# Seven block products in place of eight for the product with w_out, and two PSUM banks for the transform

## The chip, the cores and the metric

The kernel runs on one core of one Trainium2 chip. The metric is the device time of one execution in microseconds (us). The engines are named as the profile names them: PE (TensorE, matmuls; PEld its weight loads), DVE (VectorE), ACT (ScalarE), POOL (GpSimd, idle here) and SP (SyncE, which issues the transfers).

## The reference

`x` is 8 batches of 3008 tokens of 256 values, `w_in` is 256 x 2048, `w_out` is 2048 x 256.

```python
X = np.fft.rfft(x, axis=1)
Yr = Xr @ w_r - Xi @ w_i + b_r
Yi = Xr @ w_i + Xi @ w_r + b_i
Yr = sign(Yr) * max(abs(Yr) - 0.01, 0)          # Yi likewise
y = np.fft.irfft(Yr + 1j * Yi, n=3008, axis=1)
h = max(y.reshape(24064, 256) @ w_in, 0)
out = h * h @ w_out
```

## The kernel before

3008 = 47 x 64, so the transform of a batch is made of products with small tables. Stage A (`fft_a`) does the 47 points in 13 groups: `f` is folded on DVE, split into `fh` and `fl`, multiplied into `psa`, copied by ACT to `eva` and sent to a scratch in DRAM. Stage B (`fft_b`) reads it back in 12 pairs of residues per batch: `psb` is the 64-point product, `x` its copy with a sum, split into `xh` (ACT) and `xl` (DVE); the mix with w_r and w_i fills `psm1` and `psm2`; DVE makes `e` out of them in two steps, then `t` and `z` (the threshold, four pieces), and ACT and DVE the parts `zh` and `zl`; `psc` is the 64-point product back, which ACT copies to `evc` for a second scratch. The inverse 47 points (`inverse`) take two groups per chunk of tokens: `psd`, then `dv` (ACT), two pieces of `dx` (DVE) and the parts `xt`.

A float32 operand that goes through PE is split exactly into two float32r parts, `hi` on ACT and `lo` on DVE (`split`), and a product is three matmuls (`mm3`, lines L179 to L181): hi hi, lo hi and hi lo. The first batch, which has PE to itself, uses plain float32 instead.

The tokens come in 52 chunks, 48 with 470 columns and 4 with 376. For each chunk there are 16 hidden blocks `f` of 128. `moe_mm1` multiplies with w_in into the PSUM tile `ph` (6 matmuls); ACT applies relu (L484), DVE squares (L485), and `split` gives `gh` (L173) and `gl` (L174). `moe_mm2` adds the block's product with w_out to `po`, two tiles of 128 outputs (6 matmuls); it stands two blocks behind `moe_mm1` (`LAG`). After the last block `moe_out` copies `po` out, one half on ACT and one on DVE.

Each engine works through its own queue in the order of the program. That order is made by the loop over `f`: the products of the block, then pieces of the next batch's transform in the measure of the matmul time that is due (`active`, `spans`), then the product of the block two before. PSUM has eight banks: four for the transform (`ps_f`), two for `ph` (`ps_h`, one bank each, so two blocks in flight) and two for `po` (`ps_o`).

Of the kernel before, what the change touches and what calls it, by code (L numbers as in the profile page):

```python
# [30 lines left out]
P = 128  # L31
# [9 lines left out]
W = 5  # L41
# [7 lines left out]
# Upper words of 2^-127 and of float32's largest value as float64, read as float32.  # L49
# [4 lines left out]
def groups_of(b):  # L54
    """The small group comes last in an even batch and first in an odd one, so that two meet."""
    return GROUPS if b % 2 == 0 else GROUPS[-1:] + GROUPS[:-1]


def token_order(b):
    """Position in the sequence of each column: by group of n2, n1 = 0..23, then n1 = 46..24."""  # L60
    n1 = np.r_[np.arange(NR), N1 - np.arange(1, NR)]
    return np.concatenate([((64 * n1[:, None] + 47 * (g + np.arange(w))) % S).reshape(-1) for g, w in groups_of(b)])


def folded_rows():
    """Positions in the sequence that are added and subtracted, by group: n1 and 47 - n1; -1 for none."""
    n1 = np.arange(NR)[:, None]
    out = []
    for g, w in GROUPS:
        n2 = g + np.arange(w)  # L70
        a = (64 * n1 + 47 * n2) % S
        b = np.where(n1 > 0, (64 * (N1 - n1) + 47 * n2) % S, -1)
        out.append(np.stack([a, b], 2).reshape(NR * w, 2))
    return out


def _cs(num, den):
    """cos and sin of 2 pi num / den, exact at the multiples of a quarter turn."""
# [8 lines left out]
def tables():  # L87
    """Transform matrices; they depend on the shapes alone."""
# [41 lines left out]

@with_exitstack
def fft_mix_moe(ctx: ExitStack, tc: tile.TileContext, xp, w_r, w_i, b_r, b_i,
# [5 lines left out]
    sb = ctx.enter_context(tc.tile_pool(name="sb", bufs=2))  # L138
# [3 lines left out]
    ps_o = ctx.enter_context(tc.tile_pool(name="ps_o", bufs=1, space=bass.MemoryType.PSUM))  # L142

# [32 lines left out]
    def mm3(out, lt, rt, start, stop):  # L176
        """out (+)= (lt0 + lt1)^T (rt0 + rt1) in float32, by parts that one pass carries each."""
        (l0, l1), (r0, r1) = lt, rt
        nc.tensor.matmul(out, l0, r0, start=start, stop=False)  # L179
        nc.tensor.matmul(out, l0, r1, start=False, stop=False)  # L180
        nc.tensor.matmul(out, l1, r0, start=False, stop=stop)  # L181
# [43 lines left out]
    def load_w(src, dst_hi, dst_lo):  # L225
        """Yields once between the load and the work."""
        h = sb.tile([P, 512], F32, tag="zl", name="w32", bufs=2)
# [3 lines left out]
        else:  # L231
            t = sb.tile([P, 512, 2], U32, tag="xl", name="w64", bufs=2)
# [7 lines left out]
        split(h, dst_hi, dst_lo)  # L240

    def load_win():
        for c in range(DFF // 512):
            for k in range(2):
                s = slice(512 * c, 512 * c + 512)
                yield load_w(w_in[k * P:(k + 1) * P, s], wi_[0][:, k, s], wi_[1][:, k, s])

    def load_wout():
        wo_.extend(ctile(f"wo{k}", [P, NF, D], F32R) for k in range(2))
        wv = w_out.rearrange("(f p) e -> p f e", p=P)  # L250
        for f in range(0, NF, 2):
            s = slice(f, f + 2)
            yield load_w(wv[:, s, :], wo_[0][:, s, :].rearrange("p f e -> p (f e)"),
                         wo_[1][:, s, :].rearrange("p f e -> p (f e)"))

    def rolling(pieces, depth):
        """Runs the pieces one per step, their loads `depth` steps ahead."""
        q = []
        for p in pieces:
            next(p)  # L260
            q.append(p)
            if len(q) > depth:
                for _ in q.pop(0):
                    pass
                yield
        while q:
            for _ in q.pop(0):
                pass
            yield

    def ahead(n, load, depth):
        """Loads of units 0..n-1, each emitted `depth` units before its use."""
# [7 lines left out]
    # `whole`: float32 operands as they are, in the four passes of a float32 product; the first  # L280
    # batch has the tensor engine to itself, and the vector engine is spared the splits.
    def fft_a(b, whole):
# [20 lines left out]
        it = ahead(len(GROUPS), load, 6 if whole else 2)  # L303
        first = next(it)
        yield 0
        for i, t in itertools.chain([first], it):
# [3 lines left out]
            f = sb.tile([P, 512], F32, tag="fold", name="f", bufs=2)[:n]  # L310
# [3 lines left out]
            if not whole:  # L314
                fh = sb.tile([P, 512], F32R, tag="sh", name="fh", bufs=2)[:n]
                fl = sb.tile([P, 512], F32R, tag="sl", name="fl", bufs=2)[:n]
# [8 lines left out]
            if b == 0 and i % 2:  # L325
                e = sb.tile([P, 512], F32, tag="gh", name="eva", bufs=3)[:n]
# [6 lines left out]
    def fft_b(b, whole):  # L333
# [9 lines left out]
        xs, zs = {}, {}  # L343

        def stage_b(i, t):
            tv = t.rearrange("p q (k m) -> p q k m", k=2)
            ps = pst("psb").rearrange("p (k s q t) -> p k s q t", k=2, s=2, q=2)
            for k in range(2):
# [4 lines left out]
                yield 4 * 262  # L353
            x = sb.tile([P, 3, 2, P], F32, tag="x", name="x", bufs=2)
            nc.scalar.copy(x[:, 0:2].rearrange("p s k m -> p k s m"),
                           ps.rearrange("p k s q t -> p k s (q t)"))
            nc.vector.tensor_add(x[:, 2], x[:, 0], x[:, 1])
            if whole:
                xs[i] = x
            else:  # L360
                xh = sb.tile([P, 3, 2, P], F32R, tag="xh", name="xh", bufs=2)
                xl = sb.tile([P, 3, 2, P], F32R, tag="xl", name="xl", bufs=2)
# [3 lines left out]
        def stage_mix(i):  # L366
            x = xs.pop(i)
            p1, p2 = pst("psm1"), pst("psm2")
            for comp, mat, o in ((2, 0, p1[:, :D]), (1, 1, p2[:, :D]), (0, 2, p2[:, D:])):
                for k in range(2):  # L370
# [5 lines left out]
                    yield 3 * 262  # L376
# [251 lines left out]
```

## Time and profile before

| | |
|---|---|
| runs | 2694.63 us median of 3 (2693.78 to 2696.19) |
| profiled execution: span | 2694.1 us; the profile gives no other time of it |
| granted PE clock | 0.996 on average |
| first product of the tokens | starts at 123.7 us |
| HBM | 163.44 MB moved, 61 GB/s on average |

A row of a group gives line, engine, operation, out<-in by the program's names, shapes and count, then busy time, mean ns of one, and idle time of the engine before it with what ended it. A row of the timeline gives start in us, duration, engine, line and operation. A row of the chain gives start, duration and what stood there. A row of the waits says who waited for whom: us in total, times, the longest. Matmuls are pipelined: the recorded duration of one is longer than the distance to the next.

### The profile page before, as it was taken

Reading aid. Unit: us, or ns where it says so; the run is one execution under the profiler, and the core shown is the slowest. Engines: PE = TensorE matmul, PEld = TensorE weight load, DVE = VectorE, ACT = ScalarE, POOL = GpSimd, SP = SyncE. Lnnn points to the kernel's source line nnn. Section 1 sums busy time; section 2 is a strip of 40 time slices with the busy share of each in tenths; the row PEclk is TensorE's granted clock in tenths of the full one; section 3 lists DMA queues with packets and bytes.
Section 4 is the critical chain, followed back from the end, with each engine's and each line's share of the span. In section 5 each row is a group of like instructions: output and inputs, shape, how many; then the busy total and the mean of one; then the engine's idle time right before and its main releaser. Section 6 shows DMA issues by size and latency. Waiting matters only on the chain.

```text
span 2694.1 us, 37380 instructions
## 1 busy us (share of the span) xinstructions
PE 2655.6 (99%) x14088; PEld 2387.3 (89%) x14088; DVE 1841.4 (68%) x3375; ACT 1434.1 (53%) x2649; POOL 0.2 (0%) x4
## 2 busy tenths in 40 slices
PE   6899999999999999999999999999999999999999
PEld 5689989989899898998989989899899989899888
DVE  5877766767667777667676776666767677655555
ACT  5755555545555555555555554555555555444444
POOL 0000000000000000000000000000000000000000
PEclk8999999999999999999999999999999999999999
DMA  8621122111221113211032110321103211100000
GB/s 239 203 69 50 45 87 75 45 40 35 79 89 43 45 34 97 75 39 49 27 97 70 46 52 21 107 68 42 49 20 107 70 43 34 47 31 21 8 15 15
DMA packets 113240, 163.44 MB, mean 61 GB/s; under 512 B 9267, under 2 KB 72995, under 8 KB 113059
## 3 DMA queue, kind: packets, MB, share of 16 engines
q1 hardware_dynamic: 113059, 161.05, 19.3%
q8 instruction: 111, 1.82, 0.3%
q14 instruction: 70, 0.57, 0.1%
HBM read 86.04 MB, written 74.97 MB: 60 GB/s over the span
## 4 chain that ended last, share of the span: by engine, by line
PE 95%; DMA 2%; DVE 1%; ACT 1%; issue 0%; SPq 0%; ACTq 0%; DVEq 0%
PE po L179 13%; PE ph L179 13%; PE po L180 13%; PE ph L180 13%; PE po L181 13%; PE ph L181 13%; PE psd L464 3%; PE psb L351 3%; PE psm L181 2%; PE psm L179 2%; PE psm L180 2%; PE psc L180 1%; PE psc L179 1%; PE psa L179 1%; PE psa L180 1%; PE psa L181 1%
## 5 line engine op out<-in xcount | busy, mean ns | idle before, releaser
L484 ACT ACTIVATE g<-ph 128x470 f32<-128x470 f32 (+1 forms) x832 | 463.0, 557 | 636.1 <-PE ph L181 633.1
L485 DVE TENSOR_TENSOR g<-g 128x470 f32<-128x470 f32 (+1 forms) x832 | 532.2, 640 | 355.1 <-ACT g L484 351.8
L174 DVE TENSOR_TENSOR gl<-g,gh 128x470 fp32r<-128x470 f32 (+1 forms) x832 | 532.2, 640 | 310.7 <-ACT gh L173 300.3
L173 ACT CAST gh<-g 128x470 fp32r<-128x470 f32 (+1 forms) x832 | 483.6, 581 | 416.4 <-DVE g L485 411.6
L179 PE MATMUL po<-gh,wo 128*128 128x470 f32 (+1 forms) x1664 | 644.7, 388 | 0.6
L179 PE MATMUL ph<-xt,wi 128*128 128x470 f32 (+1 forms) x1664 | 622.1, 374 | 1.2 <-ACT xt L173 1.2
L180 PE MATMUL po<-gl,wo 128*128 128x470 f32 (+1 forms) x1664 | 621.5, 374 | 0.0
L180 PE MATMUL ph<-xt,wi 128*128 128x470 f32 (+1 forms) x1664 | 620.4, 373 | 0.0
L181 PE MATMUL po<-gh,wo 128*128 128x470 f32 (+1 forms) x1664 | 619.9, 373 | 0.0
L181 PE MATMUL ph<-xt,wi 128*128 128x470 f32 (+1 forms) x1664 | 617.5, 371 | 0.0
L179 PEld LDWEIGHTS ph<-xt,wi 128*128 128x128 f32 x1664 | 314.3, 189 | 39.4 <-ACT xt L173 1.6
L181 PEld LDWEIGHTS po<-gh,wo 128*128 128x128 f32 x1664 | 314.0, 189 | 38.9
L180 PEld LDWEIGHTS ph<-xt,wi 128*128 128x128 f32 x1664 | 315.8, 190 | 36.4
L181 PEld LDWEIGHTS ph<-xt,wi 128*128 128x128 f32 x1664 | 313.1, 188 | 38.4
L179 PEld LDWEIGHTS po<-gh,wo 128*128 128x128 f32 x1664 | 314.7, 189 | 30.0 <-DVE o L499 2.9
L180 PEld LDWEIGHTS po<-gl,wo 128*128 128x128 f32 x1664 | 315.0, 189 | 26.1 <-DVE gl L174 0.6
L398 DVE TENSOR_TENSOR z<-e,t 64x256 f32<-64x256 f32 x336 | 140.9, 419 | 8.1
L179 PE MATMUL psm<-wm,xh 128*128 128x256 f32 x504 | 143.6, 285 | 0.0
L181 PE MATMUL psm<-wm,xl 128*128 128x256 f32 x504 | 142.3, 282 | 0.0
L180 PE MATMUL psm<-wm,xh 128*128 128x256 f32 x504 | 142.1, 282 | 0.0
L464 PE MATMUL psd<-tD,din 120*128 120x120 f32 (+1 forms) x832 | 126.4, 275 | 5.6 <-DMA din<-s 5.6
L351 PEld LDWEIGHTS psb<-tB,bin 128*128 128x128 f32 x768 | 109.4, 194 | 24.0 <-ACT tMs L173 13.6
(75 smaller groups left out, 2317.0 us busy)
## 6 DMA issues: line engine op xcount, KB each, us to landing
bin<-s SPq DMA_DIRECT2D x96, 256.0 KB
s<-evc SPq DMA_DIRECT2D x96, 256.0 KB
s<-eva SPq DMA_DIRECT2D x96, 240.0 KB
din<-s SPq DMA_DIRECT2D x96, 240.0 KB
outT_dram<-o SPq DMA_DIRECT2D x96, 235.0 KB
xin<-in_xp_dram SPq DMA_DIRECT2D x84, 240.0 KB
w<-in_moe_w_in_dram SPq DMA_DIRECT2D x8, 512.0 KB
w<-in_moe_w_out_dram SPq DMA_DIRECT2D x8, 512.0 KB
```

Source lines behind the costliest of these rows:

```text
L173: nc.scalar.copy(hi, src)
L174: nc.vector.tensor_sub(lo, src, hi.bitcast(F32))
L179: nc.tensor.matmul(out, l0, r0, start=start, stop=False)
L180: nc.tensor.matmul(out, l0, r1, start=False, stop=False)
L181: nc.tensor.matmul(out, l1, r0, start=False, stop=stop)
L351: nc.tensor.matmul(ps[:, k, :, q, :], tv[:, q, k], tB[:, 0:r + 2:r + 1], start=True, stop=True)
L398: nc.vector.tensor_sub(z[64 * c:64 * c + 64, q], e[src, c], t[src, c])
L464: nc.tensor.matmul(ps[:, k, part], t[:, s:s + P], tD[:n, tab + part, :n], start=True, stop=True)
L484: nc.scalar.activation(g[:, :n], ph[:, :n], AF.Relu)
L485: nc.vector.tensor_mul(g[:, :n], g[:, :n], g[:, :n])
```

## The change

Two hidden blocks are now one unit `j` (`NU` = 8 per chunk). The unit's product with w_out is a product of two by two blocks: two halves of the tokens (236 and 234 columns, which share two; 188 and 188 in a small chunk) by two blocks of hidden values, and those by two halves of the outputs. It is computed by Winograd's form of Strassen's scheme, with seven block products. Their right operands are made of w_out once (`load_wout`, seven tiles per unit); their left operands `g` are four squared blocks of which three are replaced or joined by sums, with three subtractions on DVE. The seven products add up over the units of a chunk in four PSUM banks, two to a bank (`PLACES`), and are combined in `moe_out` by seven DVE instructions, which now gives four output transfers per chunk instead of two.

`ph` of a unit takes two banks and has one buffer. The transform has two banks (`ps_f`) instead of four; before the tokens' products begin it borrows `po`'s (`pst`). Square is done by ACT. Many SBUF pools are halved or shared (`tmp`, `x`, `zh`, `zl`, `xh`), and in stage B the split of `x` and the threshold are separate steps. `fill` brings in the transform's pieces twice per unit.

```diff
-    ps_f = ctx.enter_context(tc.tile_pool(name="ps_f", bufs=4, space=bass.MemoryType.PSUM))
-    ps_h = ctx.enter_context(tc.tile_pool(name="ps_h", bufs=2, space=bass.MemoryType.PSUM))
+    ps_f = ctx.enter_context(tc.tile_pool(name="ps_f", bufs=2, space=bass.MemoryType.PSUM))
+    ps_h = ctx.enter_context(tc.tile_pool(name="ps_h", bufs=1, space=bass.MemoryType.PSUM))
...
+PLACES = ((0, 0, 0), (2, 0, 1), (6, 1, 0), (5, 1, 1), (4, 2, 0), (3, 2, 1), (1, 3, 0))
+    def opnd(tag, name, dt):
+        return sb.tile([P, NPR, HALF], dt, tag=tag, name=name, bufs=2)
     def ldt(name):
-        return sb.tile([P, 512], F32, tag="ld", name=name, bufs=8)
+        return sb.tile([P, 512], F32, tag="ld", name=name, bufs=4)
     def evt(name):
-        return sb.tile([P, 512], F32, tag="ev", name=name, bufs=4)
+        return sb.tile([P, 512], F32, tag="ev", name=name, bufs=2)
...
+                a = h.rearrange("p (f e m) -> p f e m", f=2, e=2)
+                w7 = sb.tile([P, NPR, P], F32, tag="xh", name="w7")
+                nc.scalar.copy(w7[:, 0:3:2], a[:, :, 0])
+                nc.scalar.copy(w7[:, 1], a[:, 1, 1])
+                nc.vector.tensor_add(w7[:, 4], a[:, 0, 1], a[:, 1, 1])
+                nc.vector.tensor_sub(w7[:, 6], w7[:, 4], a[:, 0, 0])
+                nc.vector.tensor_sub(w7[:, 5], a[:, 0, 0], a[:, 0, 1])
+                nc.vector.tensor_sub(w7[:, 3], a[:, 1, 0], w7[:, 6])
+                split(w7, wo_[0][:, j], wo_[1][:, j])
...
+    def hidden(ph, n):
+        m, t0 = halves(n)
+        g = opnd("g", "g", F32)
+        b4 = g[:, 0:4, :m]
+        for t in range(2):
+            nc.scalar.activation(g[:, t:4:2, :m], ph[:, :, t * t0:t * t0 + m], AF.Relu)
+        nc.scalar.activation(b4, b4, AF.Square)
+        nc.vector.tensor_sub(g[:, 4:6, :m], g[:, 1:4:2, :m], g[:, 0:2, :m])
+        nc.vector.tensor_sub(g[:, 6, :m], g[:, 3, :m], g[:, 4, :m])
+        nc.vector.tensor_sub(g[:, 1, :m], g[:, 6, :m], g[:, 2, :m])
+        return g
+    def parts(g, n):
+        m, _ = halves(n)
+        gh, gl = opnd("gh", "gh", F32R), opnd("gl", "gl", F32R)
+        split(g[:, :, :m], gh[:, :, :m], gl[:, :, :m])
+        return gh, gl
-    def moe_mm2(po, gg, n, f):
-        for k in range(2):
-            es = slice(k * P, k * P + P)
-            mm3(po[k][:, :n], (wo_[0][:, f, es], wo_[1][:, f, es]),
-                (gg[0][:, :n], gg[1][:, :n]), f == 0, f == NF - 1)
+    def moe_mm2(po, gg, n, j):
+        m, _ = halves(n)
+        for s, bank, half in PLACES:
+            mm3(po[bank][:, half * m:half * m + m], (wo_[0][:, j, s], wo_[1][:, j, s]),
+                (gg[0][:, s, :m], gg[1][:, s, :m]), j == 0 and half == 0, j == NU - 1,
+                skip_group_check=True)
...
+        nc.scalar.copy(p1, p[0])
+        add, sub = nc.vector.tensor_add, nc.vector.tensor_sub
+        add(o[0][:, 0], p[2], p1)
+        add(o[0][:, 1], p[6], p1)
+        add(o[1][:, 0], p[5], o[0][:, 1])
+        add(o[0][:, 1], p[4], o[0][:, 1])
+        add(o[1][:, 1], p[4], o[1][:, 0])
+        add(o[0][:, 1], p[3], o[0][:, 1])
+        sub(o[1][:, 0], o[1][:, 0], p[1])
...
+        for j in range(NU):
+            step = c * NF + 2 * j
+            ph = moe_mm1(xts[c], n, j)
+            g = hidden(ph, n)
+            next(wout, None)
+            fill(step)
+            if len(pend) == LAG:
+                do_mm2()
+            pend.append((c, j, parts(g, n)))
+            fill(step + 1)
```

In the rows that follow, a semaphore is named by the engine that is waited for. DVE's queue before, in the middle of a batch, where the mix of a pair of residues is worked off (L381 the second step of e, L394 t, L398 z, L402 zl, L485 a square, L174 a lower part):

```order
L381 TENSOR_TENSOR e<-psm_11061,e 128x512 [waits PE_49]
L174 TENSOR_TENSOR gl<-g,gh 128x470 [waits Activation_49]
L394 TENSOR_SCALAR t<-e 128x512 [waits DVE_49]
L398 TENSOR_TENSOR z<-e,t 64x256 [waits DVE_49]
L398 TENSOR_TENSOR z<-e,t 64x256 x3
L485 TENSOR_TENSOR g<-g 128x470 [waits Activation_49]
L402 SCALAR_TENSOR_TENSOR zl<-z,sg,zh 128x256 [waits Activation_49] x2
L174 TENSOR_TENSOR gl<-g,gh 128x470 [waits PE_49,Activation_49]
```

The same place after (L430 and L431 e, L207 a lower part, L454 t, L458 z, L462 zl, L560 to L562 the three subtractions of a unit):

```order
L430 TENSOR_TENSOR e<-psm_12871,bias_82 128x512 [waits PE_49]
L207 TENSOR_TENSOR gl<-g,gh 128x1652 [waits Activation_49]
L431 TENSOR_TENSOR e<-psm_12872,e 128x512 [waits DVE_49,PE_49]
L207 TENSOR_TENSOR xl<-x,xh 128x768 [waits Activation_49]
L454 TENSOR_SCALAR t<-e 128x512 [waits DVE_49]
L458 TENSOR_TENSOR z<-e,t 64x256 [waits DVE_49]
L458 TENSOR_TENSOR z<-e,t 64x256 x3
L560 TENSOR_TENSOR g<-g 128x472 [waits Activation_49]
L462 SCALAR_TENSOR_TENSOR zl<-z,sg,zh 128x256 [waits Activation_49] x2
L561 TENSOR_TENSOR g<-g 128x236 [waits DVE_49]
L562 TENSOR_TENSOR g<-g 128x236 [waits DVE_49]
L207 TENSOR_TENSOR gl<-g,gh 128x1652 [waits Activation_49]
```

Where the threshold's pieces stood among short operations of one block each, the whole chain from e to zl now stands between one gl and the last subtraction of the next unit.

ACT's queue before, in the middle of a batch (L484 relu, L173 an upper part, L401 zh, L415 the copy evc):

```order
L484 ACTIVATE g<-ph 128x470 [waits PE_49,Activation_49]
L173 CAST gh<-g 128x470 [waits DVE_49]
L484 ACTIVATE g<-ph 128x470 [waits PE_49,Activation_49]
L401 ACTIVATE zh<-z,sg 128x256 [waits DVE_49]
L415 COPY evc<-psc 128x512 [waits DMAHW1_49,PE_49]
L401 ACTIVATE zh<-z,sg 128x256 [waits DVE_49]
L173 CAST gh<-g 128x470 [waits DVE_49]
```

The same queue after, at the unit of the DVE rows above (L558 relu, L559 square, L206 an upper part, L461 zh):

```order
L206 CAST gh<-g 128x1652 [waits DVE_49,PE_49,Activation_49]
L206 CAST xh<-x 128x768 [waits PE_49]
L558 ACTIVATE g<-ph 128x2x236 [waits PE_49]
L558 ACTIVATE g<-ph 128x2x236
L559 ACTIVATE g<-g 128x944 [waits Activation_49]
L461 ACTIVATE zh<-z,sg 128x256 [waits DVE_49] x2
L206 CAST gh<-g 128x1652 [waits DVE_49,PE_49,Activation_49]
L558 ACTIVATE g<-ph 128x2x236 [waits PE_49]
```

One gh now covers all seven operands of a unit and waits for DVE's subtractions and for the product two units before (PE), and the next unit's relu stands behind it.

More of the change, by code (lines that the diff above doesn't have):

```diff
@@ L160, in fft_mix_moe, with tmp @@
     wo_ = []
+    starting = [True]
+    turn = itertools.count()
     def ldt(name):
-        return sb.tile([P, 512], F32, tag="ld", name=name, bufs=8)
+        return sb.tile([P, 512], F32, tag="ld", name=name, bufs=4)
     def evt(name):
-        return sb.tile([P, 512], F32, tag="ev", name=name, bufs=4)
+        return sb.tile([P, 512], F32, tag="ev", name=name, bufs=2)
+    def tmp(name):
+        return sb.tile([P, 512], F32, tag="tmp", name=name, bufs=2)
     def pst(name):
+        k = next(turn) % 6
+        if starting[0] and k > 1:
+            return ps_o.tile([P, 512], F32, tag=f"o{k - 2}", name=name)
         return ps_f.tile([P, 512], F32, tag="f", name=name)
@@ L239, in load_w @@
             narrow(t, h)
-        split(h, dst_hi, dst_lo)
+        use(h)
     def load_win():
@@ L245, in load_win, with use, rolling @@
                 s = slice(512 * c, 512 * c + 512)
-                yield load_w(w_in[k * P:(k + 1) * P, s], wi_[0][:, k, s], wi_[1][:, k, s])
+                def use(h, k=k, s=s):
+                    split(h, wi_[0][:, k, s], wi_[1][:, k, s])
+                yield load_w(w_in[k * P:(k + 1) * P, s], use)
     def load_wout():
-        wo_.extend(ctile(f"wo{k}", [P, NF, D], F32R) for k in range(2))
+        wo_.extend(ctile(f"wo{k}", [P, NU, NPR, P], F32R) for k in range(2))
         wv = w_out.rearrange("(f p) e -> p f e", p=P)
[L251 to L258, printed above, removed]
+        for j in range(NU):
+            def use(h, j=j):
+                a = h.rearrange("p (f e m) -> p f e m", f=2, e=2)
[7 more added lines that the diff above has]
+                split(w7, wo_[0][:, j], wo_[1][:, j])
+            yield load_w(wv[:, 2 * j:2 * j + 2, :], use)
+    def rolling(pieces):
+        last = None
         for p in pieces:
+            if last is not None:
+                for _ in last:
+                    pass
             next(p)
[L261 to L268, printed above, removed]
+            last = p
             yield
+        for _ in last:
+            pass
+        yield
     def ahead(n, load, depth):
@@ L301, in load @@
                 return st[i // 8][:NR * GROUPS[i][1], i % 8, :]
-        it = ahead(len(GROUPS), load, 6 if whole else 2)
+        it = ahead(len(GROUPS), load, 3 if b == 1 else 2)
         first = next(it)
@@ L324, in fft_a @@
                         (fh[:, cs], fl[:, cs]), True, True)
-            if b == 0 and i % 2:
-                e = sb.tile([P, 512], F32, tag="gh", name="eva", bufs=3)[:n]
+            if b == 0 and i % 3:
+                e = sb.tile([P, NPR * HALF], F32, tag="g", name="eva", bufs=2)[:n, :512]
             else:
@@ L423, in fft_b @@
                 _, t = next(it)
-                yield from stage_b(i, t)
-            if 0 <= i - 1 < NPAIR:
-                yield from stage_mix(i - 1)
+                stage_b(i, t)
+                yield 8 * 262
+            if 0 <= i - 2:
+                stage_c(i - 2)
+                yield 3 * 518
+            e = None
+            if 0 <= i - 1 < NPAIR:
+                e = stage_mix(i - 1)
+            if i < NPAIR:
+                split_x(i)
+            if e is not None:
+                threshold(i - 1, e)
+                yield 18 * 262
             if i >= NPAIR:
                 yield 0
-            if 0 <= i - 2:
-                yield from stage_c(i - 2)
     GAP = 8
@@ L489, in moe_mm2, with moe_mm1 @@
[L489 to L493 removed]
+            yield 8 * 262
+    def moe_mm1(xt, n, j):
+        ph = ps_h.tile([P, 2, 512], F32, tag="h", name="ph")
+        for a in range(2):
+            f = 2 * j + a
+            fs = slice(f * P, f * P + P)
+            for k in range(2):
+                mm3(ph[:, a, :n], (wi_[0][:, k, fs], wi_[1][:, k, fs]),
+                    (xt[0][:, k, :n], xt[1][:, k, :n]), k == 0, k == 1)
+        return ph
@@ L495, in moe_out @@
     def moe_out(c, po):
         n = cols[c]
+        m, t0 = halves(n)
+        p = {s: po[bank][:, half * m:half * m + m] for s, bank, half in PLACES}
+        p1 = sb.tile([P, HALF], F32, tag="p1", name="p1")[:, :m]
+        o = [sb.tile([P, 2, HALF], F32, tag=f"o{k}", name="o") for k in range(2)]
+        o = [x[:, :, :m] for x in o]
+        nc.scalar.copy(p1, p[0])
+        add, sub = nc.vector.tensor_add, nc.vector.tensor_sub
+        add(o[0][:, 0], p[2], p1)
+        add(o[0][:, 1], p[6], p1)
@@ L553, in fft_mix_moe, with fill @@
     LAG = 2
-    def do_mm2():
-        c, f, gg = pend.pop(0)
-        if f == 0:
-            pos[c] = [ps_o.tile([P, 512], F32, tag=f"o{k}", name=f"po{k}") for k in range(2)]
-        moe_mm2(pos[c], gg, cols[c], f)
-        if f == NF - 1:
+    def fill(step):
+        for b, (s0, s1) in spans.items():
+            if s0 == step:
+                active.append([full(b), s0, s1, 0, A_COST + 1000 * GAP + B_COST])
+        for a in list(active):
+            gen, s0, s1, done, total = a
+            want = total * (step + 1 - s0) / (s1 - s0)
+            while a[3] < want or step >= s1:
+                try:
+                    a[3] += next(gen)
+                except StopIteration:
+                    active.remove(a)
+                    break
+    def do_mm2():
+        c, j, gg = pend.pop(0)
+        if j == 0:
+            pos[c] = [ps_o.tile([P, 512], F32, tag=f"o{k}", name=f"po{k}") for k in range(4)]
+        moe_mm2(pos[c], gg, cols[c], j)
+        if j == NU - 1:
             moe_out(c, pos.pop(c))
```

124 lines of the change are left out of this document (57 added, 67 removed).

## The prediction

> **What bounds the kernel now.** I read the busy shares first, then the chain that ended last, then the waits, then the timeline.
>
> ```profile
> span 2694.1 us, 37380 instructions
> PE 2655.6 (99%) x14088; PEld 2387.3 (89%) x14088; DVE 1841.4 (68%) x3375; ACT 1434.1 (53%) x2649; POOL 0.2 (0%) x4
> ...
> PE 95%; DMA 2%; DVE 1%; ACT 1%; issue 0%; SPq 0%; ACTq 0%; DVEq 0%
> ...
> L179 PE MATMUL ph<-xt,wi x1664: 329/377/482, 123.7 to 2685.5; 128*128 128x470 f32 x170, 128*128 128x376 f32 x15
> ...
> ACT g L484 <- PE ph L181: 633.1, 722, 2.3
> DVE g L485 <- ACT g L484: 351.8, 494, 2.2
> DVE gl L174 <- ACT gh L173: 300.3, 503, 1.0
> ```
>
> PE makes up 95% of the chain; DVE and ACT wait for it and for each other, and both have room. The token products run from 123.7 us to the end. Matmul durations overlap, so PE's price is the distance between starts, or the chain's share of each:
>
> ```profile
> 1003.05 0.37 PE L181 MATMUL ph<-xt,wi 128*128 128x470 f32 x1
> 1003.26 0.28 PE L179 MATMUL psm<-wm,xh 128*128 128x256 f32 x1
> 1003.38 0.28 PE L180 MATMUL psm<-wm,xh 128*128 128x256 f32 x1
> 1003.50 0.28 PE L181 MATMUL psm<-wm,xl 128*128 128x256 f32 x1
> 1003.62 0.38 PE L179 MATMUL po<-gh,wo 128*128 128x470 f32 x1
> ...
> 1010.07 0.23 PE psc L181
> 1010.30 0.44 PE psd L464 x4
> ...
> 180.85 0.89 PE psb L351 x8
> ```
>
> 470 columns cost 0.2125 us, 256 cost 0.118, so 0.44 ns a column and 5 ns beside. By that, 376 columns cost 0.171 us.
>
> I count in units, a pair of hidden blocks f, of which there are 416: 384 with 470 columns, 32 with 376. A unit before is 24 matmuls: 5.10 us, or 4.10 in a small one; together 2089. The transform adds on PE, per pair of residues (84 behind the start), 0.89 + 18 x 0.118 + 3 x 0.23 = 3.7 us, 312; per group of stage A (78) 6 x 0.118 = 0.71, 55; per chunk (52) 16 psd at 0.11 = 1.76, 92. With 124 of start and 8 of end this is 2680 of the 2694.1 us profiled. That execution lies 0.5 us below the runs' median.
>
> **What the change does to PE.** The product with w_out becomes 21 matmuls of 236 columns in place of 12 of 470. By the line above 236 columns cost 0.109 us, so 2.29 us instead of 2.55; in small units 188 columns cost between 0.088 and 0.109, for the weight load need not shrink. PE alone would come to 384 x 4.84 + 32 x 4.15 + 312 + 55 + 92 + 155 = 2606 us. No float32r matmul narrower than 256 stands in this trace; that it keeps to the line is the choice nearest to the row.
>
> **What it does to ACT and DVE.** The durations come from these rows:
>
> ```profile
> L484 ACT ACTIVATE g<-ph 128x470 f32<-128x470 f32 x768 | 432.0, 563 | 600.2 <-PE ph L181 598.0 <-ACT xt L173 0.2
> L173 ACT CAST gh<-g 128x470 fp32r<-128x470 f32 x768 | 451.1, 587 | 381.3 <-DVE g L485 377.3
> L173 ACT CAST xh<-x 128x768 fp32r<-128x768 f32 x84 | 70.1, 835 | 1.7 <-DVE x L357 0.5
> L174 DVE TENSOR_TENSOR gl<-g,gh 128x470 fp32r<-128x470 f32 x768 | 497.0, 647 | 284.9 <-ACT gh L173 276.7 <-PE po L180 2.0 <-PE ph L181 1.3
> L174 DVE TENSOR_TENSOR xl<-x,xh 128x768 fp32r<-128x768 f32 x84 | 80.4, 957 | 10.1 <-ACT xh L173 7.0
> L471 DVE TENSOR_TENSOR dx<-psd,dv 128x230 f32<-128x230 f32 x96 | 37.3, 388 | 0.0
> ...
> 2640.11 0.56 ACT L484 ACTIVATE g<-ph 128x470 f32<-128x470 f32 x1 [0.69 <-PE ph L181]
> 2640.71 0.65 DVE L485 TENSOR_TENSOR g<-g 128x470 f32<-128x470 f32 x1 [0.60 <-ACT g L484]
> 2641.39 0.59 ACT L173 CAST gh<-g 128x470 fp32r<-128x470 f32 x1 [0.72 <-DVE g L485]
> ```
>
> ACT costs 0.832 ns an element more and DVE 1.04; a hand-over between them costs some 0.035 us. Per unit after: two relus of 472 elements, 1.13; the square of 944 moves from DVE to ACT, 587 + 474 x 0.832 = 0.98; the cast gh of 1652, 1.57. On DVE: the three new subtractions, 0.65 + 0.39 + 0.39; gl of 1652, 1.88. So ACT rises from 2.30 to 3.68 us a unit and DVE from 2.59 to 3.31, while PE falls by 0.26.
>
> What decides is the order. In ACT's queue each unit reads relu, relu, square, gh, and the next unit's relu stands behind gh. gh is one instruction over all seven operands, so it waits for the last subtraction, and that for the square. This is a ring: 1.13 + 0.98 + 1.43 + 1.57 = 5.11, five hand-overs add 0.18, neighbours on ACT that overlap take back 0.13 (row at 1010.64 below): **5.16 us a unit**, 4.37 in a small one (relu 0.484 each, the others by the same slopes). PE cannot run ahead of it by more than a unit: there is one pair of PSUM banks for ph, so the next unit's first product waits for this unit's relus. Before, ph had two buffers, and the order relu, gh of one f at a time left ACT idle for 2.55 - 1.15 us each. Units together: 384 x 5.16 + 32 x 4.37 = 2121, which is 32 above PE's 2089 before. Thus the matmuls saved are gone already without any transform.
>
> **The transform inside the ring.** Its rows:
>
> ```profile
> 1008.89 0.42 DVE L394 TENSOR_SCALAR t<-e 128x512 f32<-128x512 f32 x1
> 1009.35 1.74 DVE L398 TENSOR_TENSOR z<-e,t 64x256 f32<-64x256 f32 x4
> 1011.12 0.65 DVE L485 TENSOR_TENSOR g<-g 128x470 f32<-128x470 f32 x1
> 1011.68 0.48 DVE L402 SCALAR_TENSOR_TENSOR zl<-z,sg,zh 128x256 fp32r<-128x256 f32 x1
> ...
> 1010.23 0.51 ACT L401 ACTIVATE zh<-z,sg 128x256 fp32r<-128x256 f32 x1
> 1010.64 0.57 ACT L415 COPY evc<-psc 128x512 f32<-128x512 f32 x1
> ...
> L381 DVE TENSOR_TENSOR e<-psm,e 128x512 f32<-128x512 f32 x96 | 66.1, 688 | 43.1 <-PE psm L181 41.7 <-PE psm L372 1.3
> L355 ACT COPY x<-psb 128x512 f32<-128x512 f32 x96 | 55.9, 582 | 11.7 <-PE psb L351 11.7
> ```
>
> A DVE instruction that waits for nothing starts 0.09 us before its forerunner's recorded end, one on ACT 0.10. In the unit with the mix, DVE's queue reads gl, e, xl, t, four z, first subtraction, two zl, two subtractions; then comes gh. From one start of gh to the next: 1.60 for gh, 1.79 gl, 0.60 e, 0.87 xl, 0.46 t, 1.77 z, 0.56, 0.78 zl, 0.86 with the last hand-over: 9.29 us, 4.13 over the ring. Only the other e lies under gh, at no cost. The copies x and evc stand on ACT between gh and square: 0.48 each. So a pair of residues costs 5.1 us, 428 in all; on PE it cost 3.7, beside which DVE's part was hidden. If all of it hid under DVE's and ACT's idle time it would cost nothing.
>
> ```profile
> L469 ACT COPY dv<-psd 128x240 f32<-128x240 f32 x96 | 34.3, 357 | 21.0 <-PE psd L464 21.0
> L173 ACT CAST xt<-dx 128x470 fp32r<-128x470 f32 x96 | 56.4, 587 | 24.9 <-DVE dx L471 22.2
> L499 DVE COPY o<-po 128x470 f32<-128x470 f32 x48 | 30.9, 643 | 5.4 <-PE po L181 5.4
> L329 ACT COPY eva<-psa 120x512 f32<-120x512 f32 x96 | 56.1, 587 | 29.5 <-PE psa L181 9.8 <-PE psa L321 9.6 <-DMA s<-eva 6.2
> L173 ACT CAST fh<-f 120x512 fp32r<-120x512 f32 x72 | 44.8, 623 | 2.8 <-DVE f L312 2.8
> ```
>
> Each half of the inverse puts two dx between the subtractions and xt ahead of gh: 1.0 us (0 if all under gh, 2.4 if none). Writing out a chunk was one copy on ACT and one on DVE; now it is a copy and seven sums of 236, at 0.43 in a chain, six of them beside gh's 1.6 us: 1.2. A chunk thus costs 3.2, 166 in all. A group of stage A costs ACT 1.0 for fh and eva; its bounds are 0.7 (PE's own) and 2.4, all of DVE's work too, and I take 1.2, near the rows: 94. w_out's seven combinations go through the ring in eight pieces, about 3 us each: 24.
>
> At the start only four buffers in place of seven take stage A's results; three waits like the longest s<-eva, 7 us, would make 21 (0 to 40): 145. SP issues two more output transfers a chunk, which nothing waits for. The half-size pools for ev and ld cost nothing at one eviction in 5 us; otherwise they add to the second rival. The last unit ends with gl, 21 matmuls, the sums and a transfer: 12.
>
> Sum: 145 + 2121 + 428 + 94 + 166 + 24 + 12 = **2990 us**, 11% slower.
>
> **The rivals.**
> - *The work packs well and PE stays the bound*: 2606 us. For it: DVE's 1841 us grow by some 410, ACT's 1434 by about 560, both below 2606. It decides at 2694, where 296 of the 712 us that I charge to transform, chunks and w_out would have to hide in idle time. Against it: queues keep their order, and in the unit with the mix nothing but one e stands under gh.
> - *Two PSUM banks for the transform*: PE stops at psd or psm until DVE has read e, with the next ph queued behind. 1.5 us for each of 84 pairs and 104 psd would give 3270; half of it 3130. PE's slack in the ring speaks against it: 0.3 us in a bare unit, 2.3 in the one with the mix (9.29 against 4.84 + 2.12).
> - *Narrow float32r falls to float32's passes*: the first batch's float32 psm give its price.
>
> ```profile
> 94.81 1.67 PE L372 MATMUL psm<-wmf,x 128*128 128x256 f32 x7
> ...
> L179 PEld LDWEIGHTS psm<-wm,xh 128*128 128x128 f32 x504 | 94.9, 188 | 8.5
> ```
>
> Six starts in 1.30 us, two a product, make 0.43 us for 256 columns, 0.40 for 236: 8.4 us for the 21 instead of 2.29, some 5100 us. No row below 256 excludes it.
> - *Weight loads set the pace*: at 0.188 us one after the other, 8736 loads in place of matmuls at 0.109 would lift PE from 2606 to 3300. The psm rows 0.118 apart, each with its load, speak against it. The Trainium skill, "Perfetto Trace Analysis", section "Identifying the Most-Contended Engine", calls matmul busy time a bad measure and takes the summed time of LDWEIGHTS slices over the window as the good one; by that rule the 17,832 loads after would not fit into the time before. The trace bears it out only in part: 14,088 loads of this length sum to 98% of the span, yet loads overlap each other where matmuls are short.
>
> **How the numbers follow.** The ring, my forecast, gets 0.75, with its own range 2820 to 3130 from the bounds of the pair, the groups and the start. Good packing 0.12, the PSUM banks 0.08, narrow passes 0.03, weight loads 0.02. A range of 2690 to 3180 leaves out the good packing, the last two and a part of the banks, 2 in 10. About 0.2% is what a measurement of this kernel can tell from no change: faster 0.12, the same 0.02, slower 0.86.
>
> **What would show it.** Right: PE's share of the span falls to about 85%, with idle time ahead of ph released by ACT's relu; in the last chunks relus of successive units stand 5.2 us apart; square about 0.98, gh 1.57, gl 1.88 us; gaps of 1.5 us on ACT ahead of gh, ended by the last subtraction; 9 us between gh's around z. Wrong: po starts more than 0.12 us apart, PE at 97% or more, or PE waiting at psd and psm for DVE's e.

## The result and the profile after

The changed kernel takes 3065.5 us (median of 4 runs, 3063.7 to 3065.6) against 2694.6 us for the kernel before, run beside it: 1.137 times as long, with a 95% interval of 1.135 to 1.139. The forecast was 2990 us, with 2690 to 3180 as its range. The profiled execution has a span of 3063.6 us.

In the new kernel's lines L558 is relu, L559 the square, L560 to L562 the three subtractions, L206 the cast to the high part (gh, xh, fh, xt), L207 the subtraction for the low part (gl, xl), L212 to L214 the three matmuls of a product, L461 zh and L458 z. The page begins its parts with the span, the busy shares and the chain that ended last:

```profile
span 3063.6 us, 45137 instructions
...
PE 2758.2 (90%) x17832; PEld 2523.0 (82%) x17832; DVE 2247.4 (73%) x3719; ACT 1914.9 (63%) x2665; POOL 0.2 (0%) x4
...
DVE 39%; ACT 32%; PE 16%; issue 10%; DMA 3%; ACTq 0%; SPq 0%; DVEq 0%
ACT gh L206 14%; ACT g L559 7%; ACT g L558 6%; DVE g L560 6%; DVE gl L207 6%; DVE z L458 4%; DVE g L561 4%; DVE g L562 4%; PE ph L212 2%; DVE xl L207 2%; PE ph L213 2%; PE ph L214 2%; DVE e L431 2%; PE po L212 2%; PE po L214 2%
```

PE's share of the chain fell from 95 to 16%, though PE is still "busy" for 90% of the span: a matmul is drawn 0.27 or 0.37 us long where the next could start 0.111 or 0.2125 us behind it, so a wait shorter than the difference does not show as idle time. The chain now passes through the relus, the square, the three subtractions and gh, which is the order in which a unit goes through them. The waits (us in all, times, longest) name the same members:

```profile
DVE gl L207 <- ACT gh L206: 530.1, 365, 3.4
ACT gh L206 <- DVE g L562: 525.0, 312, 2.8
ACT zh L461 <- DVE z L458: 186.7, 164, 4.1
...
PE ph L212 <- ACT g L558: 71.2, 53, 4.6
PE psa L212 <- ACT fh L206: 52.2, 27, 4.3
ACT eva L375 <- PE psa L214: 50.5, 33, 2.5
...
PE psd L531 <- DVE e L430: 12.3, 8, 2.0
```

ACT waits for DVE's last subtraction and DVE waits for ACT's cast, 525 and 530 us. Each has more than a quarter of the span idle, and each waits for the other. The timeline of a unit without transform, near the end, shows how:

```profile
3000.76 1.58 ACT L206 CAST gh<-g 128x1652 fp32r<-128x1652 f32 x1 [1.68 <-DVE g L562]
3002.23 1.01 ACT L558 ACTIVATE g<-ph 128x472 f32<-128x472 f32 x2
3002.36 1.88 DVE L207 TENSOR_TENSOR gl<-g,gh 128x1652 fp32r<-128x1652 f32 x1 [1.72 <-ACT gh L206]
3003.28 0.99 ACT L559 ACTIVATE g<-g 128x944 f32<-128x944 f32 x1
3004.30 0.65 DVE L560 TENSOR_TENSOR g<-g 128x472 f32<-128x472 f32 x1
3004.99 0.40 DVE L561 TENSOR_TENSOR g<-g 128x236 f32<-128x236 f32 x1
3005.43 0.41 DVE L562 TENSOR_TENSOR g<-g 128x236 f32<-128x236 f32 x1
3005.94 1.57 ACT L206 CAST gh<-g 128x1652 fp32r<-128x1652 f32 x1 [1.67 <-DVE g L562]
```

From gh to gh it is 5.18 us. Leave gl out, and every row starts within 0.11 us of its forerunner's end; the hand-overs go ACT, DVE, ACT. That is the ring; gl alone lies beside it, as does all of PE's work. In a unit with the threshold the same stretch is 9.40 us, because DVE's queue holds other work ahead of the subtractions for which gh waits:

```profile
1004.62 1.57 ACT L206 CAST gh<-g 128x1652 fp32r<-128x1652 f32 x1 [1.67 <-DVE g L562]
...
1006.23 1.88 DVE L207 TENSOR_TENSOR gl<-g,gh 128x1652 fp32r<-128x1652 f32 x1 [1.11 <-ACT gh L206]
1008.02 0.68 DVE L431 TENSOR_TENSOR e<-psm,e 128x512 f32<-128x512 f32 x1
1008.62 0.95 DVE L207 TENSOR_TENSOR xl<-x,xh 128x768 fp32r<-128x768 f32 x1
1009.49 0.42 DVE L454 TENSOR_SCALAR t<-e 128x512 f32<-128x512 f32 x1
1009.94 1.74 DVE L458 TENSOR_TENSOR z<-e,t 64x256 f32<-64x256 f32 x4
1011.71 0.65 DVE L560 TENSOR_TENSOR g<-g 128x472 f32<-128x472 f32 x1
1012.28 0.88 DVE L462 SCALAR_TENSOR_TENSOR zl<-z,sg,zh 128x256 fp32r<-128x256 f32 x2
...
1014.02 1.57 ACT L206 CAST gh<-g 128x1652 fp32r<-128x1652 f32 x1 [1.79 <-DVE g L562]
```

### The profile page after: what moved, and what is told of

It reads as the page before. It is cut to its first block, busy times and chain, and to the rows that moved or that the text cites. A ratio compares the mean times of both kernels' runs of the same rounds, so it can differ in the third digit from the quotient of the medians.

```text
span 3063.6 us, 45137 instructions
## 1 busy us (share of the span) xinstructions
PE 2758.2 (90%) x17832; PEld 2523.0 (82%) x17832; DVE 2247.4 (73%) x3719; ACT 1914.9 (63%) x2665; POOL 0.2 (0%) x4
## 4 chain that ended last, share of the span: by engine, by line
DVE 39%; ACT 32%; PE 16%; issue 10%; DMA 3%; ACTq 0%; SPq 0%; DVEq 0%
ACT gh L206 14%; ACT g L559 7%; ACT g L558 6%; DVE g L560 6%; DVE gl L207 6%; DVE z L458 4%; DVE g L561 4%; DVE g L562 4%; PE ph L212 2%; DVE xl L207 2%; PE ph L213 2%; PE ph L214 2%; DVE e L431 2%; PE po L212 2%; PE po L214 2%
## 5 line engine op out<-in xcount | busy, mean ns | idle before, releaser
L207 DVE TENSOR_TENSOR gl<-g,gh 128x1652 fp32r<-128x1652 f32 (+1 forms) x416 | 770.3, 1852 | 530.1 <-ACT gh L206 530.1
L206 ACT CAST gh<-g 128x1652 fp32r<-128x1652 f32 (+1 forms) x416 | 644.7, 1550 | 585.6 <-DVE g L562 525.0
L212 PE MATMUL po<-gh,wo 128*128 128x236 f32 (+1 forms) x2912 | 827.1, 284 | 34.6 <-DVE o L588 16.8
L213 PE MATMUL po<-gl,wo 128*128 128x236 f32 (+1 forms) x2912 | 813.9, 280 | 3.3 <-DVE gl L207 3.3
L214 PE MATMUL po<-gh,wo 128*128 128x236 f32 (+1 forms) x2912 | 814.6, 280 | 0.0
L212 PE MATMUL ph<-xt,wi 128*128 128x470 f32 (+1 forms) x1664 | 652.6, 392 | 72.0 <-ACT g L558 71.2
L214 PE MATMUL ph<-xt,wi 128*128 128x470 f32 (+1 forms) x1664 | 630.0, 379 | 0.0
L212 PEld LDWEIGHTS po<-gh,wo 128*128 128x128 f32 x2912 | 569.0, 195 | 64.5 <-DVE o L588 19.0
L213 PEld LDWEIGHTS po<-gl,wo 128*128 128x128 f32 x2912 | 569.3, 195 | 11.2 <-DVE gl L207 4.1
L214 PEld LDWEIGHTS po<-gh,wo 128*128 128x128 f32 x2912 | 571.1, 196 | 0.0
L558 ACT ACTIVATE g<-ph 128x472 f32<-128x472 f32 (+1 forms) x832 | 418.3, 554 | 97.3 <-PE ph L214 96.8
L212 PEld LDWEIGHTS ph<-xt,wi 128*128 128x128 f32 x1664 | 322.8, 194 | 123.4 <-ACT g L558 91.5
L559 ACT ACTIVATE g<-g 128x944 f32<-128x944 f32 (+1 forms) x416 | 410.6, 987 | 8.6
L214 PEld LDWEIGHTS ph<-xt,wi 128*128 128x128 f32 x1664 | 322.9, 194 | 40.4
L560 DVE TENSOR_TENSOR g<-g 128x472 f32<-128x472 f32 (+1 forms) x416 | 266.7, 641 | 103.6 <-ACT g L559 93.2
L461 ACT ACTIVATE zh<-z,sg 128x256 fp32r<-128x256 f32 x168 | 85.6, 510 | 186.7 <-DVE z L458 186.7
L212 PE MATMUL psm<-wm,xh 128*128 128x256 f32 x504 | 147.1, 292 | 40.3 <-DVE dx L537 22.5
L562 DVE TENSOR_TENSOR g<-g 128x236 f32<-128x236 f32 (+1 forms) x416 | 165.7, 398 | 11.4
L561 DVE TENSOR_TENSOR g<-g 128x236 f32<-128x236 f32 (+1 forms) x416 | 165.1, 397 | 8.7
L458 DVE TENSOR_TENSOR z<-e,t 64x256 f32<-64x256 f32 x336 | 141.0, 420 | 7.4
```

The lines of the kernel that those rows point to most:

```text
L206: nc.scalar.copy(hi, src)
L207: nc.vector.tensor_sub(lo, src, hi.bitcast(F32))
L212: nc.tensor.matmul(out, l0, r0, start=start, stop=False, **kw)
L213: nc.tensor.matmul(out, l0, r1, start=False, stop=False, **kw)
L214: nc.tensor.matmul(out, l1, r0, start=False, stop=stop, **kw)
L458: nc.vector.tensor_sub(z[64 * c:64 * c + 64, q], e[src, c], t[src, c])
```

## The experiments

Theory: the ring of relu, square, subtractions and gh over two in-order queues sets the pace, and the transform that stands in those queues is added to it. Rivals: PE's own work; the two PSUM banks; the sum of work on ACT and DVE, in whatever order. Each kernel was timed in three rounds beside the kernel before, which measured 2694.4 to 2696.4 us.

**Less work for PE.** The changed kernel with the third matmul of each w_out product left out, so that w_out's low part does not enter the result: 14 matmuls a unit in place of 21.

```
-            mm3(o, (wo_[0].., wo_[1]..), (gg[0].., gg[1]..), ...)
+            nc.tensor.matmul(o, wo_[0].., gg[0].., ...)
+            nc.tensor.matmul(o, wo_[0].., gg[1].., ...)
```

> The changed kernel with one of the three passes left out in the product with w_out (the pass with the low part of w_out), 14 matmuls of 236 columns a unit in place of 21. The output lacks that pass. The ring on ACT and DVE (theory): PE loses 7 x 0.111 = 0.78 us a unit, 320 us of work, but stands in no ring, so a bare unit stays at 5.19 us and the time falls by 0 to 50 us, to 3015 to 3065. PE or the narrow matmuls as the bound (rival): the time falls by some 320 us, to about 2745. Stops at the two PSUM banks (rival): PE's stops at psd and psm stay, the time falls by 100 to 200 us, since PE has less to do behind each stop.

3063.1 us, 1.137 (1.135 to 1.138): no change. The page's busy shares, and one of the waits:

```profile
PE 2534.2 (83%) x14920; PEld 2264.7 (74%) x14920; DVE 2240.8 (73%) x3719; ACT 1913.5 (63%) x2665; POOL 0.2 (0%) x4
```

```profile
PE ph L212 <- ACT g L558: 232.9, 152, 5.1
```

2912 matmuls at 0.111 us, some 320 us of PE's work, went away, and PE's wait for the relus rose from 71 to 233 us. PE is not the bound. The Trainium skill, "Perfetto Trace Analysis", section "Identifying the Most-Contended Engine", prefers the summed weight loads to the matmuls' busy time for telling how near PE is to its limit. This case does not bear that out: the loads' times sum to 99% of the span in the kernel before, to 114% in the changed kernel and to 98% here, and PE is the bound in the first of the three alone (the shares on the page, 89, 82 and 74%, count loads that overlap once).

**The order of the queues.** Two ways to take gh off the ring. In the first, the split of a unit is issued one unit later, behind the next unit's square, so that gh no longer stands between a unit's subtractions and the next relu; g keeps its two buffers:

```
+            if held:
+                pc, pj, pg = held.pop()
...
+                with tc.issue_after(sq):
+                    gg = parts(pg, cols[pc])
...
+            held.append((c, j, g))
```

> The changed kernel with the split into gh and gl put one unit later, behind the next unit's square on ACT; nothing is left out. gh no longer waits for the subtractions of its own unit. g still has two buffers, so the next relu has to wait until gl has read the older one. The ring (theory): the old ring is gone and a new one stands in its place, relu 1.03, square 0.99, gh 1.57, gl 1.88 and hand-overs, 5.55 us in a bare unit in place of 5.19; the time is between 3000 and 3250. The sum of work on ACT and DVE as the bound (rival): the same work, so 3065 and 5.19. PE as the bound (rival): 3065.

3078.4 us, 1.142 (1.141 to 1.144). The timeline near the end, and its largest wait:

```profile
3022.08 1.02 ACT L558 ACTIVATE g<-ph 128x472 f32<-128x472 f32 x2 [2.00 <-DVE gl L207]
3023.13 0.99 ACT L559 ACTIVATE g<-g 128x944 f32<-128x944 f32 x1
3024.03 1.56 ACT L206 CAST gh<-g 128x1652 fp32r<-128x1652 f32 x1
3027.59 1.02 ACT L558 ACTIVATE g<-ph 128x472 f32<-128x472 f32 x2 [2.00 <-DVE gl L207]
```

```profile
ACT g L558 <- DVE gl L207: 611.0, 324, 4.1
```

The old ring is gone, gh follows the square at once, and another took its place: the relu waits until gl has read g two units back. 5.51 us a unit. The same with a third buffer for g (paid for with one load buffer and with p1 in a shared one):

```
-        return sb.tile([P, NPR, HALF], dt, tag=tag, name=name, bufs=2)
+        return sb.tile([P, NPR, HALF], dt, tag=tag, name=name, bufs=3 if tag == "g" else 2)
```

> The same late split with three buffers of g (room for it is made by three load buffers in place of four, two loads ahead at the start in place of three, and p1 among the temporaries), so that neither gh nor the next relu waits for DVE's last step. The ring (theory): no ring is left that is longer than PE's unit of 2.55 + 21 x 0.111 = 4.88 us, and the transform is once more beside PE where DVE keeps up: 2620 to 2800. Two PSUM banks (rival): the transform's stops stay as they are, above 2950. The sum of work on ACT and DVE (rival): unchanged work, 3065. Narrow matmuls (rival): PE no faster than now, 3065.

2841.3 us, 1.054 (1.053 to 1.056): 224 us less than the changed kernel, though 41 us above what I had expected at most. The second way leaves the order and cuts the one cast in four, so that ACT casts the blocks that are ready while DVE still subtracts:

```
-        split(g[:, :, :m], gh[:, :, :m], gl[:, :, :m])
+        for s in (slice(0, 3, 2), slice(3, 6), slice(6, 7), slice(1, 2)):
+            nc.scalar.copy(gh[:, s, :m], g[:, s, :m])
+        nc.vector.tensor_sub(gl[:, :, :m], g[:, :, :m], gh[:, :, :m].bitcast(F32))
```

> The changed kernel with gh cast in four instructions, blocks 0 and 2 first, then 3 to 5, 6, 1, each waiting only for its own subtraction; ACT has about 0.6 us more work a unit. The ring (theory): the casts run beside the subtractions, relu 1.03, square 0.99 and casts 2.3 make 4.3 us, so that a bare unit comes to PE's 4.88, and the unit with z falls from 9.40 to about 8.2: 2820 to 2940. The sum of work on ACT and DVE as the bound (rival): ACT's extra work makes it slower, 3065 to 3300. PE as the bound (rival): 3065.

2809.7 us, 1.042 (1.041 to 1.044), 10 us below the range that I gave, at 148 us more work on ACT. Busy shares and chain, then two relus of its timeline in the last third:

```profile
PE 2658.2 (95%) x17832; PEld 2469.4 (88%) x17832; DVE 2243.4 (80%) x3719; ACT 2063.1 (74%) x3913; POOL 0.2 (0%) x4
...
PE 73%; DVE 14%; ACT 8%; DMA 3%; issue 3%; SPq 0%; DVEq 0%; ACTq 0%
```

```profile
2500.31 1.02 ACT L558 ACTIVATE g<-ph 128x472 f32<-128x472 f32 x2 [0.63 <-PE ph L214]
...
2505.21 1.02 ACT L558 ACTIVATE g<-ph 128x472 f32<-128x472 f32 x2 [0.65 <-PE ph L214]
```

The relus stand 4.90 us apart and wait for PE: 12 x 0.2125 + 21 x 0.111 is 4.88. Three lines, with the same products, banks and sums, give back 256 of the 371 us. That settles the ring, and with it that the sum of work is not the cause: ACT does more here and the kernel is faster.

**The two PSUM banks alone.** The kernel before, with nothing but

```
-    ps_f = ctx.enter_context(tc.tile_pool(name="ps_f", bufs=4, space=bass.MemoryType.PSUM))
+    ps_f = ctx.enter_context(tc.tile_pool(name="ps_f", bufs=2, space=bass.MemoryType.PSUM))
```

> The kernel before, with one thing of the change alone: the transform gets two PSUM banks instead of four, and nothing uses the other two. Ring theory: the banks are a side matter; the new kernel's waits on PE at psd, psb and psm for a reader of a bank sum to some 30 us. With PE as the bound here they cost about that: 2725 us, between 2695 and 2760. Rival (the banks are the cause): 1.5 us for each of 84 pairs and 104 halves of the inverse, or half of it: 2835 to 2975 us.

2703.8 us against 2694.4: 1.004 (1.002 to 1.005). The banks cost 9 us where PE is the bound and the order is that of the kernel before.

**Stage A.** Its price was the worst term of my sum (below). In the changed kernel its split, its products and its eviction were put into three successive steps of the loop:

```
+                split(f, fh, fl)
+                if late:
+                    evict(*late)
+                yield 3 * 262
...
+                late = (g, w, n, o, i)
+                yield 3 * 262
```

> The changed kernel with one edit: stage A's split, products and eviction of a group stand in three successive steps of the loop, so that the eviction no longer stands in ACT's queue right behind the cast whose products it waits for. If ACT's wait for psa (50 us in all) and PE's for fh (52 us) are why a group costs 1.8 us and not the 1.2 that I had taken: 3015 us, between 3000 and 3035. If a group's price is the work on ACT and DVE that stands in the ring, whatever its order: 3055 to 3070 us.

3036.1 us, 1.127 (1.125 to 1.129): 29 us of the 50 expected, just above the range that I gave. Its waits show which part did not come: ACT's for psa fell from 50.5 to 11.8 us, but PE's for fh only from 52.2 to 36.6, its wait for fl rose from 14.6 to 24.4, and fh itself now waits for the products to release its one buffer:

```profile
PE psa L212 <- ACT fh L206: 36.6, 24, 4.3
...
ACT fh L206 <- PE psa L214: 17.3, 18, 2.3
...
ACT eva L359 <- PE psa L214: 11.8, 12, 2.2
```

**Towards the kernel before.** Four versions build on gh in pieces. First all of the transform in smaller portions: stage A as above, and the mix, the split of x and the halves of the threshold each in a step of its own,

```
-                yield 18 * 262
+                yield 6 * 262      (behind the mix)
+                yield 4 * 262      (behind the split of x, and in each half of the threshold)
```

> The cast of gh in four pieces, and the transform handed out in smaller portions: stage A's split, products and eviction in three successive steps, the mix, the split of x and the two halves of the threshold each in a step of their own, with buffers of their own for e and t. If what is left over the pieces' 2810 us is portions that stand together in one unit, stage A falls from 1.8 to about 1.2 us a group (48 us) and some 20 to 30 us go elsewhere: 2740 us, between 2700 and 2780. If what is left is PE's own work (bare unit 4.90, mix 2.14, both near PE's own price), it stays within 2790 to 2815. Neither theory says that it beats the kernel before: 2695 us lies only 90 above PE's own sum.

2821.2 us, 1.047 (1.046 to 1.049), slower than the pieces alone by 11.5 us and above both forecasts. I reckon PE's gaps behind the start from the trace, as the sum over its matmuls of the distance to the next start beyond that kind's own price (0.2125 us for ph, 0.111 for po, 0.118 for psm and psa, and so on), where that is over 0.05. They are 162 us in the run with pieces, 86 of them at psa; here 175, with 63 at psa. (Counted against each kind's median distance instead, they are some 20 us more in every run, with the same differences.) What stage A gave, other places took: ph behind po went from 10 to 25.

Then stage A alone, in steps and with its share of the schedule tripled, so that its groups stand about one in two units:

```
-    A_COST = len(GROUPS) * 6 * 262
+    A_COST = len(GROUPS) * 18 * 262
```

> The pieces of gh, with stage A's three steps, and stage A's share of the schedule tripled, so that its groups stand about one in two units instead of several in one. In the run with pieces PE's gaps beside psa sum to some 85 us behind the start. If these are the crowding of stage A, most of them go: 2740 us, between 2720 and 2770. If a group's price stays wherever it stands, nothing is won: 2795 to 2815 us.

2773.8 us, 1.029 (1.027 to 1.031), 36 us less and 4 above the range. The gaps at psa fell from 86 to 29 us; those within psm rose from 7 to 19, and psc and psb gained 20 beside it. To this was added, in the first batch, that stage A evicts into its own input:

```
-            if b == 0 and i % 3:
-                e = sb.tile([P, NPR * HALF], F32, tag="g", name="eva", bufs=2)[:n, :512]
+            if b == 0:
+                e = load(i)
```

> The same, and in the first batch stage A writes its result over the group's input instead of into one of four shared buffers. The changed kernel's first token product stands 23 us later than before; if the four buffers make that, most of it goes: 15 to 25 us under the run without this. If it is something else of the start, no change. Together with the thin stage A 2720 us, still above the kernel before.

2763.9 us, 1.025 (1.023 to 1.027), 10 us less where I had expected 15 to 25. The first and last ph of the run without it and of this one:

```profile
L212 PE MATMUL ph<-xt,wi x1664: 328/377/954, 150.0 to 2759.8; 128*128 128x470 f32 x170, 128*128 128x376 f32 x15
```

```profile
L212 PE MATMUL ph<-xt,wi x1664: 328/377/954, 138.6 to 2748.2; 128*128 128x470 f32 x170, 128*128 128x376 f32 x15
```

So the buffers make 11 of the 23 to 26 us by which the start is late; the rest is not explained. Last, the fourth step of the transform was issued behind the threshold, with two buffers for zh and zl:

```
-            if 0 <= i - 2:
+            if whole and 0 <= i - 2:
                 stage_c(i - 2)
...
+            if not whole and 0 <= i - 2:
+                stage_c(i - 2)
+                yield 3 * 518
```

> The last one, with the fourth step of the transform (psc, evc) issued behind the threshold instead of ahead of the mix, and two buffers in place of one for zh and zl (and so for fh and fl). In the run before it PE loses some 125 us in gaps behind the start: about 19 between the mix's products, 29 beside psa, 18 ahead of or within psc, 9 behind psb. If buffers and the order of the two banks make these, half goes: 2700 us, between 2680 and 2740; only at the low end does it reach the kernel before. If the queues of ACT and DVE make them, it stays at 2750 to 2770.

2783.5 us, 1.033 (1.031 to 1.035): 20 us slower. The gaps within psm rose from 19 to 30 us, and 13 behind po ahead of it are 7 more than before; the gaps in all from 126 to 147. That lies outside both forecasts. The edit changes the order and the buffers together, so it shows only that this order with these buffers is worse. The waits point to the two banks: PE's waits for a reader of one of the transform's banks rose from some 28 us (psm for evc 14.6, psc for dx 7.6, and smaller ones) to some 50 (psm for dx 14.8, x 9.3 and evc 8.9, psb for evc 12.7, and smaller ones), about as much as the time. Whether the number of banks makes these waits or the queue in which the reader stands, no run separates.

No version beats the kernel before. The best, at 2762.9 us of span, nearly adds up: PE's own 2606, which already holds a later start (the prediction's 155 us for start and end, here 153); 16 because a product of 236 columns takes 0.111 and not 0.109 us; 8 because one of 188 columns in a small chunk takes 0.11 too; and 126 of gaps. That makes 2756, 7 short, as the same sum was 14 short for the kernel before (2680 of 2694). At the measured spacings the units alone fall from 2089 to 2014 us of PE's time, so the seven products save 75 us. The gaps and a start that is 15 us later take 141, which is 66 more; the span is 69 longer. What the seven products take away in slack costs more than they save in every order tried.

## Why the prediction was right, by its steps

- **PE bounds before, the ring after**: right. The run with less work on PE and the one with gh in pieces show it from two sides.
- **The ring's length**: 5.16 us forecast; 5.18 from gh to gh above. The new instructions' sizes came out of the slopes of the old rows (0.98, 1.57 and 1.88 forecast), as the groups by form show:

```profile
L207 DVE TENSOR_TENSOR gl<-g,gh 128x1652 fp32r<-128x1652 f32 x384 | 721.4, 1879 | 499.1 <-ACT gh L206 499.1
L206 ACT CAST gh<-g 128x1652 fp32r<-128x1652 f32 x384 | 603.3, 1571 | 546.5 <-DVE g L562 490.4 <-PE po L214 19.8 <-PE ph L214 12.1
...
L559 ACT ACTIVATE g<-g 128x944 f32<-128x944 f32 x384 | 383.9, 1000 | 7.7
```

- **The unit with the mix**: 9.29 forecast, 9.40 above, and DVE's queue in the order that the prediction listed. A least-squares fit of all intervals between gh's by what stands in them charges 404 us to the pairs of residues (428 forecast). The fit is an estimate: with other rows counted in the intervals the pairs come to between 334 and 413 us, and what they lose goes to the units.
- **Stage A**: the mis-sized term. I took 1.2 us a group, "near the rows", between bounds of 0.7 and 2.4; the fit gives 1.83, that is 142 us and not 94 (135 to 158 with other rows counted). I had counted the work of fh and eva and no wait. In ACT's queue eva stood behind the fh for whose products it waits, and PE stood at fh. Taking ACT's part of that away gave 29 us.
- **Chunks**: 180 us by the fit against 166 (158 to 204 with other rows counted); **w_out** 16 against 24; **the start**: the first ph at 146.6 us against 145. The fit gives the units 2151 and not 2121, but not all of that is theirs: the 76 large units with nothing of the transform between their gh's take 5.19 us on average and the six small ones 4.38, which makes 2133. The rest is transform that the fit cannot tell from the units. By the fit, units (+30), stage A (+48) and chunks (+14), less pairs (-24) and w_out (-8), are 60 of the 74 us that the span lies above the sum; the rest is at the start, the end and between the fit's terms. Stage A is the one term that stays above its forecast whatever rows are counted.
- **Two PSUM banks, 3130 to 3270**: rightly put low. Alone they cost 9 us. In the changed kernel PE's waits for a reader of one of the transform's banks come to some 69 us (psm for dx 22.5 and evc 16.1, psd for e 12.3, psc for x 11.6, and smaller ones), but PE has slack there; in the best version, where it has little, to some 28. So the banks did not make the kernel slower, and yet they are part of what keeps the best version above 2606.
- **Narrow products and weight loads**: the prices that they named, 0.40 and 0.188 us, are both refuted by the spacing of the w_out products, 236 columns each, in the timeline: 0.111 us, each with its load. The signs named (PE at 97%, po more than 0.12 us apart) did not come.

```profile
3001.29 0.27 PE L212 MATMUL po<-gh,wo 128*128 128x236 f32 x1
3001.40 0.27 PE L213 MATMUL po<-gl,wo 128*128 128x236 f32 x1
3001.51 0.28 PE L214 MATMUL po<-gh,wo 128*128 128x236 f32 x1
```

But the prediction's line of 0.44 ns a column does not go on below that. The products of 188 columns in a small chunk stand 0.11 us apart as well, just above the 0.088 to 0.109 that I had allowed for them:

```profile
2768.11 0.27 PE L214 MATMUL po<-gh,wo 128*128 128x188 f32 x1
2768.22 0.28 PE L212 MATMUL po<-gh,wo 128*128 128x188 f32 x1
2768.34 0.27 PE L213 MATMUL po<-gl,wo 128*128 128x188 f32 x1
```

In a row of such products, each with a weight load of its own, the price thus does not fall below 0.11 us here, and 236 columns lie just at that floor (by the line, 0.11 us is some 240 columns). By this a scheme with still narrower products would win next to nothing more on PE; that is an estimate, and whether the load makes the floor or something else no run shows.

- **PE's share at about 85%**: it reads 90%. That sign was ill chosen, since short waits hide in the modelled ends of matmuls; the chain's 16% says it better.
- **Good packing, 2606 us**: false for the order as written, and also the end that no reordering reached: 2764 at best.

## What to carry to other kernels

When work moves from a saturated engine to two half-idle ones, follow one operand through both queues and add up the instructions between its two passes of the same point. If that loop is longer than the saturated engine's unit, it is the new time, whatever the busy shares say. One large instruction over all operands is cheap on its engine and dear in such a loop: cut in pieces it cost 148 us more of ACT here and saved 256 us of time. And a deeper order without a buffer to match (the late split with two buffers) only trades one ring for another.

## What the runs showed of the hardware

I had not reckoned with the clock. Its mean was 0.996 before, 0.959 after, 0.930 with a third of w_out's matmuls left out and 0.985 in the best version. It goes by PE's long waits rather than by their sum: the version with the smaller portions has 13 us more of gaps than the pieces alone, but 9 gaps above 2 us where those have 16, and its clock is higher, 0.980 against 0.976. Behind the unit with the mix shown above PE has a gap of 2.1 us (no matmul starts between 1014.4 and 1016.5). The changed kernel in windows of 1 us there (length, each engine's busy time, then the granted clock as the first number behind POOL's):

```profile
1014.00:1015.00 1.00, 0.42 (x4) 0.23 (x3) 0.00 (x0) 0.98 (x1) 0.00 (x0) 1.00 0.00 0
1015.00:1016.00 1.00, 0.00 (x0) 0.00 (x0) 0.38 (x1) 1.00 (x3) 0.00 (x0) 1.00 0.01 2
1016.00:1017.00 1.00, 0.45 (x2) 0.42 (x3) 1.00 (x1) 0.97 (x3) 0.00 (x0) 1.00 0.56 147
1017.00:1018.00 1.00, 1.00 (x5) 0.85 (x4) 0.94 (x2) 0.53 (x1) 0.00 (x0) 0.57 0.31 113
1018.00:1019.00 1.00, 1.00 (x4) 0.82 (x3) 0.93 (x3) 0.00 (x0) 0.00 (x0) 0.50 0.00 0
1019.00:1020.00 1.00, 1.00 (x4) 0.87 (x3) 0.09 (x1) 0.80 (x1) 0.00 (x0) 0.50 0.00 0
```

The clock falls to one half some 0.6 us after the work has come back (0.57 in the window from 1017 is one half from 1017.1 on), and the 2 us that follow the last row have 0.86, one half until 1020.6. So this gap of 2.1 us costs PE another 1.7. Not every gap does. Behind the first product of the tokens, the changed kernel has 11 gaps between 2.0 and 2.5 us, and a fall of the clock follows 8 of them within 3.5 us; it follows 10 of the 54 between 1 and 2 us, and 20 of the 21 longer ones. While the ring sets the pace nobody waits for the slower clock: the run with a third of w_out's matmuls left out took at 0.930 the time that the changed kernel took at 0.959. In the versions near PE's bound the slow stretches are part of the gaps that ate the saving. Behind the first product of the tokens the clock is at one half for 88 us in the run with pieces and for 47 in the best version, so that it can make at most 44 and 24 us of their 162 and 126 us of gaps (an estimate: half of each stretch). The Trainium skill, "TensorE: Matmul & The Clock Gate", Part 1, puts the fall to half rate behind an idle window of some 3.4 us; that the rate is one half the trace bears out, while here a gap of 2.1 us was enough.
